# First expert of an attention and mixture-of-experts kernel: its third weight chunk is loaded behind two token gathers, the rest behind five, and the next expert's choices start behind two tiles' remainders

## The chip, the core and the metric

The kernel runs on one core of a Trainium2 chip. The metric is the device time of one execution in microseconds (us), of which a median of some runs is taken. The engines named below are PE (TensorE, matrix products; PEld is its load of stationary operands), DVE (VectorE), ACT (ScalarE), POOL (GpSimd) and SP (SyncE, which here only issues DMAs). POOL issues DMAs too. In the DMA tables q1 holds what SP issues and q0 (software_dynamic) what POOL issues.

## The reference, cut to what matters

```python
attn_out = _attn_ref(q, k, v)          # 8 x 8 heads, 576 positions, window of 64
x = attn_out.transpose(0, 2, 1, 3).reshape(4608, 512)
logits = x @ w_gate                    # 8 experts
order = np.argsort(-logits.flatten())
for idx in order:                      # best pair first
    tok, e = idx // 8, idx % 8
    if assigned[tok] >= 0 or counts[e] >= 576: continue
    assigned[tok] = e; counts[e] += 1
for e in range(8):
    mask = assigned == e
    h = np.maximum(x[mask] @ w1[e], 0.0)   # 512 -> 1024
    out[mask] = h @ w2[e]                  # 1024 -> 512
```

Each expert gets exactly 576 tokens, given out greedily by descending score, so the experts are settled one after another: an expert's tokens are known once the threshold score at which it fills up is found, with all earlier experts' tokens taken out.

## The kernel before

The first part computes attention and writes its rows to a buffer `xs` in device memory. The second part, which the change concerns, has three interwoven strands for each expert p = 0 to 7.

**Routing** (`Routing.steps`). On DVE the *choices* (L772, L554 to L561) find each token's best expert that is left. ACT copies the result into `one4` (L782). Then eight *rounds* (`search`) narrow the threshold: DVE compares (`G`, L586), PE counts (nine products, L632), DVE picks the next digit. A list of the token numbers follows (`listing`: products L911 or L909, L921), and its last step writes `idx` (L927). Expert 0 has a shorter search of its own (`first`).

**Loading** (`Experts.load`). An expert's weights come in eight chunks of 512 KB (128 x 1024 floats): 0 to 3 of w1, 4 to 7 of w2. Each is loaded into `st` (L993). ACT rounds it to `wh` (L1016) and writes `wl` = -`wh` (L1030), and an adding DMA of POOL's queue adds `st` to `wl` (L1032), which leaves the rounding error in `wl`. Expert 0's chunk 0 takes a subtraction on DVE (L1044) in place of the adding DMA. Before the change expert 0's chunks 0 to 3 are issued by SP and 4 to 7 by POOL.

**Tokens and products** (`Experts.turn`, `Experts.steps`). POOL gathers the tokens in five indirect DMAs (L1085): four tiles of 128 rows into `xg` and a last one of 64 into `rest`. PE transposes each tile (`tp`, four products, L1104), ACT rounds it to `xh` (L1074) and DVE writes the remainder beside it (L1078; *remainders* or *lows* in the code). Products of expert 0 (`h`, L1166) come in units of twelve: four of `wh` with the rounded tokens, four of `wl`, four of `wh` with the remainders. A unit needs 128 columns of a weight chunk, so two units need one chunk. The first six units (chunks 0 to 2) take the first 256 tokens, then the same six take the other 320, then chunk 3's. ACT writes each unit's result to `hh` (L1130) and DVE its remainder to `hl` (L1135); three buffers `h` go round. The second layer is `o` (L1200, L1210), and a scatter of POOL's queue writes the rows out (L1189). Where PE has nothing to do at the start, small products of no use keep it busy (`warm`, L593): 28 behind expert 0's list and 6 behind its first tile.

The order on each engine is fixed when the program is written out. Generators wait in a queue (`Streams`) under a clock that is a guess of times, and the instruction of the earliest goes down next. So the guessed times (`there`, `ADDED`, `GATHER` and so on) set which instruction stands ahead of which, and every engine then works strictly through its list.

Of the kernel before, what the change touches and what calls it, by code (L numbers as in the profile page):

```python
# [444 lines left out]
class Routing:  # L445
# [316 lines left out]
    def steps(self, p):  # L762

        nc, wk, V = self.nc, self.wk, self.V
# [5 lines left out]
        if p < E - 1:  # L770
            if p:
                for f in self.choices(0, NJ, p):  # L772
                    f()
                    yield self.dve(490)
# [16 lines left out]
            q = tile_([128, NJ], FT, name="q")  # L791
# [70 lines left out]
    def listing(self, p, Y, slack):  # L862

        nc = self.nc
# [34 lines left out]
        for j0, j1 in ((0, NJ),) if p else ((0, 18), (18, 36)):  # L899
            n = j1 - j0  # L900
# [22 lines left out]
        if p == 0:  # L923
            self.warm(28)
        yield self.busy(255) + 200 + slack
# [17 lines left out]

GATHER = 4200
PLAIN, ADDING, TOKENS, LAND, FETCH = 1350, 2650, 700, 2000, 3600
ADDED = 4500
# [5 lines left out]
class Experts:  # L952
    def __init__(self, ctx, tc, c, xs, w1, w2, out, ring=8):
# [11 lines left out]
        self.first = 0  # L965
        self.gathered = 0
        self.sent = 0
        self.turned = 0
# [12 lines left out]
    def load(self, p, ei):  # L981
# [7 lines left out]
        def fetch(i):  # L989
            st[i] = fw.tile([128, 1024], FT, name="st", bufs=STAGE)  # L990

            q, r = (nc.gpsimd, eg) if p == 0 and i >= 4 else (nc.sync, e)
            q.dma_start(st[i], self.part(i, r))  # L993

            t = self.clock() + self.busy(PLAIN, "dma") + (LAND if i else FETCH)
            if p == 0:
                t = max(self.clock(), there.get(i - 1, 0)) + 1500 * (1 if i else 2)
            if p == 0 and i == 4:

                t = max(t, self.clock() + self.busy(0, "pool") + FIRST)  # L1000
            there[i] = t

        ahead = 3 if p else 4
        for i in range(ahead):
            fetch(i)
        if p == 0:
            yield lambda: self.gathered
        for i in range(2 * NCH):
# [10 lines left out]
            if not (p and quick):  # L1019
                yield lambda: self.gathered > p  # L1020
            if p == 0 and i == 0:
# [6 lines left out]
            else:  # L1028

                nc.scalar.activation(lo, hi.bitcast(FT), AF.Copy, scale=-1.0)  # L1030
                yield self.busy(1050, "act") + 100
                nc.gpsimd.dma_start(lo.bitcast(FT), st[i], accum_op=OP.add)  # L1032
                t = self.busy(650, "pool")
                t = max(t + 350 + ADDING, self.busy(ADDING, "dma")) + LAND if p else t + ADDED - 1200
                self.spawn(self.ready(p, i, hi, lo), t)
                dt = 1300
            self.taken += 1
            for n in () if p == 0 and i < 2 else (4, 5, 6) if p == 0 and i == 2 else (i + ahead,):
                if n < 2 * NCH:
                    fetch(n)  # L1040
# [22 lines left out]
    def turn(self, p, idx):  # L1063
# [18 lines left out]
        g = [g[:, a] for a in range(4)] + [self.rest]  # L1082
        for a in range(5):
            n = 128 if a < 4 else 64
            nc.gpsimd.indirect_dma_start(out=g[a][0:n], out_offset=None, in_=self.xs,  # L1085
                                         in_offset=IndirectOffsetOnAxis(ap=idx[0:n, a:a + 1], axis=0))
            self.busy(TOKENS, "dma")
        if not p:
            self.begun = self.clock()
        self.gathered += 1  # L1090
        there = self.clock() + self.busy(6400, "pool") + GATHER
        yield lambda: self.first == p
        self.XT[p] = x = fw.tile([128, NX, 2 * CAP], FR, name="xh")
        for tiles in ((0, 1), (2, 3), (4,)) if p else ((0,), (1,), (2,), (3,), (4,)):
            yield max(0, there - 1280 * (4 - tiles[-1]) - self.clock())
            if p > 1:
# [4 lines left out]
            for n, a in enumerate(tiles):  # L1101
# [4 lines left out]
                self.spawn(evac(a, 128 if a < 4 else 64, t), dt + 150 + 700 * n)  # L1106
            if p == 0 and a < 1:
                self.warm(6)
# [144 lines left out]
def body(tc, q, k, v, vt, wg, w1, w2, xs, out):  # L1253
    nc = tc.nc
    with ExitStack() as ctx:
# [10 lines left out]
        ex = Experts(ctx, tc, c, xs, w1, w2, out)  # L1266
        rt.spare, rt.joined = ex.room, ex.join

# [44 lines left out]
```

## Time and profile before

| | |
|---|---|
| median of three runs | 632.21 us (628.75 to 632.36) |
| the profiled execution | 634.6 us, of which its span is 632.8 us |
| PE busy over the span | 601.8 us (95%), 5968 products |
| DVE, ACT, POOL busy | 457.6, 371.5 and 188.0 us |
| mean granted clock of PE | 0.982 of full speed |

The profiled execution took 1.8 us more than its span, and 2.4 us more than the median. The span is read in stages: attention up to some 152 us, expert 0's routing up to 168 us, and then the eight experts. Where PE works without a gap, a stage is as long as PE's own list of instructions; where it has a gap, the last wait in front of the gap sets the time.

### The profile page before, as it was taken

How to read it: one execution, taken by the hardware profiler on the slowest of the kernel's cores; microseconds unless marked ns; L12 is line 12 of the kernel's file. 1: busy time of each engine (PE TensorE's matmuls, PEld its weight loads, DVE VectorE, ACT ScalarE, POOL GpSimd, SP SyncE). 2: the span in 40 equal slices, each digit the busy share in tenths (PEclk: the TensorE clock that was granted, in tenths of full speed). 3: DMA queues.
4: the chain of work that ended last, by engine and by line, in shares of the span. 5: the costliest groups of instructions: out<-in, count | busy, mean ns of one | idle time of the engine just before them, and what ended most of it. 6: DMA issues, size and time to landing. Idle time of an engine off the chain costs nothing.

```text
span 632.8 us, 16208 instructions
## 1 busy us (share of the span) xinstructions
PE 601.8 (95%) x5968; PEld 512.4 (81%) x5968; DVE 457.6 (72%) x2151; ACT 371.5 (59%) x798; POOL 188.0 (30%) x244
## 2 busy tenths in 40 slices
PE   8999999996589999999999999999999999999996
PEld 6677777885489878878988997898889779888984
DVE  6888888887678869877986897798789646714410
ACT  6788888996365177357636735564664536514310
POOL 1324453341241162045107204420621460011011
PEclk9999999998689999999999999999999999999999
DMA  9999999942597199379829927983994798210001
GB/s 318 332 364 366 370 388 385 347 159 73 184 235 157 47 320 244 74 258 231 195 89 291 247 58 272 221 191 117 252 230 86 277 242 304 67 41 35 2 25 51
DMA packets 44945, 128.82 MB, mean 204 GB/s; under 512 B 4672, under 2 KB 5312, under 8 KB 44864
## 3 DMA queue, kind: packets, MB, share of 16 engines
q1 hardware_dynamic: 30736, 79.52, 35.1%
q0 software_dynamic: 13840, 47.72, 32.5%
q8 instruction: 48, 0.79, 0.5%
q10 hardware_dynamic: 288, 0.52, 0.3%
q14 instruction: 33, 0.27, 0.1%
HBM read 82.14 MB, written 18.87 MB: 160 GB/s over the span
## 4 chain that ended last, share of the span: by engine, by line
PE 52%; issue 17%; DMA 2%; POOL 2%; DVE 2%; ACT 1%; another core or an unknown queue 0%; POOLq 0%; DVEq 0%
PE h L1166 25%; PE o L1210 18%; PE o L1200 4%; PE rps L632 2%; DMA wl<-st 2%; POOL out L1189 2%; PE tp L1104 2%; PE rps L593 1%; PE rps L909 1%; DMA xs<-x 0%; ACT xh L1074 0%; DVE xh L1078 0%; PE rps L911 0%; POOLq L1309 0%
## 5 line engine op out<-in xcount | busy, mean ns | idle before, releaser
L1166 PE MATMUL h<-xh,wh 128*128 128x320 f32 (+2 forms) x800 | 161.9, 334 | 1.8 <-ACT xh L1074 1.8
L1166 PEld LDWEIGHTS h<-xh,wh 128*128 128x128 f32 x800 | 125.2, 190 | 6.7 <-ACT xh L1074 1.9
L1189 POOL DMA_INDIRECT out<-ot,idx x40 | 42.2, 1055 | 244.9 <-DVE ot L1187 98.2
L1210 PE MATMUL o<-wh,hh 128*128 128x512 f32 x256 | 101.2, 395 | 0.0
L1210 PE MATMUL o<-wh,hl 128*128 128x512 f32 x256 | 100.9, 394 | 0.0
L1210 PE MATMUL o<-wl,hh 128*128 128x512 f32 x256 | 100.7, 393 | 0.0
L141 ACT ACTIVATE pe<-st,mx 128x128 f32<-128x128 f32 x288 | 92.0, 393 | 5.9 <-DVE mx L136 5.8
L1166 PE MATMUL h<-xh,wl 128*128 128x256 f32 (+1 forms) x512 | 92.1, 299 | 0.0
L1166 PEld LDWEIGHTS h<-xh,wl 128*128 128x128 f32 x512 | 79.3, 189 | 4.4
L136 DVE CUSTOM_DVE_ANT_0 st<-Sp,mask 128x128 f32<-128x128 f32 x288 | 63.8, 285 | 8.2 <-PE Sp L128 7.2
L1016 ACT ACTIVATE wh<-st 128x1024 fp32r<-128x1024 f32 x64 | 67.4, 1054 | 2.8 <-DMA st<-w 2.8
L1032 POOL DMA_DIRECT2D wl<-st x51 | 46.3, 976 | 64.5 <-ACT wl L1030 23.6
L1180 ACT ACTIVATE ot<-o 128x512 f32<-128x512 f32 x32 | 19.1, 597 | 75.2 <-PE o L1210 68.6
L1210 PEld LDWEIGHTS o<-wh,hl 128*128 128x128 f32 x256 | 48.1, 188 | 9.5
L1210 PEld LDWEIGHTS o<-wl,hh 128*128 128x128 f32 x256 | 48.1, 188 | 9.5
L1210 PEld LDWEIGHTS o<-wh,hh 128*128 128x128 f32 x256 | 48.1, 188 | 9.2
L1030 ACT ACTIVATE wl<-wh 128x1024 fp32r<-128x1024 f32 x51 | 53.9, 1057 | 0.6
L1127 DVE TENSOR_TENSOR sum<-h,sum 128x256 f32<-128x256 f32 x56 | 23.3, 415 | 37.3 <-ACT sum L1125 36.7
L1130 ACT ACTIVATE hh<-h 128x320 fp32r<-128x320 f32 (+1 forms) x72 | 30.9, 430 | 29.1 <-PE h L1166 28.2
L150 ACT ACTIVATE pt<-Tp 128x512 f32<-128x512 f32 x72 | 42.2, 588 | 9.8 <-PE Tp L148 9.6
L176 PE MATMUL Op<-VO,pt 128*64 128x73 f32 x608 | 43.3, 230 | 3.4 <-issue 2.9
L176 PEld LDWEIGHTS Op<-VO,pt 128*64 128x64 f32 x608 | 37.6, 136 | 8.3 <-issue 3.7
(207 smaller groups left out, 1095.9 us busy)
## 6 DMA issues: line engine op xcount, KB each, us to landing
st<-w SPq DMA_DIRECT2D x60, 512.0 KB
wl<-st POOLq DMA_DIRECT2D x51, 512.0 KB
xs<-x SPq DMA_DIRECT2D x36, 256.0 KB
VO<-v SPq DMA_DIRECT2D x6, 1168.0 KB
Q<-q SPq DMA_DIRECT2D x6, 1152.0 KB
K<-k SPq DMA_DIRECT2D x6, 1152.0 KB
VT<-vt SPq DMA_DIRECT2D x6, 1152.0 KB
VO<-v SPq DMA_DIRECT2D x4, 584.0 KB
```

The source lines that it names most:

```text
L136: nc.vector.tensor_tensor_reduce(st[:, h, :], Sp[h % 2][:, h // 2], mk, scale=-0.125, scalar=3.0e38, op0=OP.add, op1=OP.min, accum_out=mx[ ...
L141: nc.scalar.activation(pe[:, h, :], st[:, h, :], AF.Exp, bias=mx[:, h:h + 1], scale=-1.0)
L150: return pt, lambda: nc.scalar.activation(pt.rearrange("p h q -> p (h q)"), Tp, AF.Copy)
L176: nc.tensor.matmul(Op[g][64 * a:64 * a + 64, h, :], pt[:, h, 64 * a:64 * a + 64], vv[a][:, 4 * g + h, :], start=True, stop=True)
L1016: nc.scalar.activation(hi, st[i], AF.Copy)
L1030: nc.scalar.activation(lo, hi.bitcast(FT), AF.Copy, scale=-1.0)
L1032: nc.gpsimd.dma_start(lo.bitcast(FT), st[i], accum_op=OP.add)
L1130: nc.scalar.activation(hh[:, f, c0:c1], h, AF.Relu)
L1166: nc.tensor.matmul(h[:, 0:w], wv[:, cc, 128 * (f % 2):128 * (f % 2) + 128], x[:, cc, x0:x0 + w], start=(k == 0), stop=(k == 4 * len(terms) ...
L1189: nc.gpsimd.indirect_dma_start(out=self.out[5 * p + a], out_offset=IndirectOffsetOnAxis(ap=idx[0:m, a:a + 1], axis=0), in_=ot[0:m], in_off ...
L1200: nc.tensor.matmul(o, hh[:, f, 512:], w[:, 512 * (f % 2):512 * (f % 2) + 512], start=(f == 0 and n == 0), stop=(f == NF - 1 and n == 1))
L1210: nc.tensor.matmul(o, ht[:, f, 128 * a:128 * a + 128], wt[:, 512 * (f % 2):512 * (f % 2) + 512], start=(k == 0), stop=(k == 23))
```

## The change

- `load`: for expert 0, SP issues chunks 0 and 1 alone. Chunk 2 is issued by POOL once two gathers have been issued (`got > 1`), and chunks 3 to 6 by POOL once chunk 2 has been handled.
- `turn`: for expert 0, two gathers are issued first; the other three wait until one adding DMA has been issued (`added`). The guessed times of the tiles are written out anew.
- `steps` of the routing: expert 1's choices wait until two tiles' remainders stand in DVE's list (`begin`).
- `warm`: 17 in place of 28 behind expert 0's list, and 6 behind the second tile as well as the first.

```diff
@@ Routing.steps
             if p:
+                if p == 1:
+                    yield self.begin
                 for f in self.choices(0, NJ, p):
@@ Routing.listing
-            self.warm(28)
+            self.warm(17)
@@ Experts.load
-            q, r = (nc.gpsimd, eg) if p == 0 and i >= 4 else (nc.sync, e)
+            q, r = (nc.gpsimd, eg) if p == 0 and i >= 2 else (nc.sync, e)
...
+            if p == 0 and i == 2:
+                t = self.clock() + SECOND_CHUNK
...
-        ahead = 3 if p else 4
-        for i in range(ahead):
+        ahead = 3
+        for i in range(ahead if p else 2):
             fetch(i)
         if p == 0:
-            yield lambda: self.gathered
+            yield lambda: self.got > 1
+            fetch(2)
...
-                yield lambda: self.gathered > p
+                yield lambda: (self.got > 1 if i < 2 else self.gathered) if p == 0 else self.gathered > p
...
                 nc.gpsimd.dma_start(lo.bitcast(FT), st[i], accum_op=OP.add)
+                self.added += 1
...
-            for n in () if p == 0 and i < 2 else (4, 5, 6) if p == 0 and i == 2 else (i + ahead,):
+            for n in () if p == 0 and i < 2 else (3, 4, 5, 6) if p == 0 and i == 2 else (i + 4 - (p > 0),):
@@ Experts.turn
-        for a in range(5):
+        def get(a):
             n = 128 if a < 4 else 64
             nc.gpsimd.indirect_dma_start(...)
             self.busy(TOKENS, "dma")
-        if not p:
+            self.got += 1
+        def others():
+            yield lambda: self.added
+            for a in range(2, 5):
+                get(a)
+            self.gathered += 1
+            self.busy(3900, "pool")
+        for a in range(2 if p == 0 else 5):
+            get(a)
...
+                yield lambda: self.gathered or a0 < 2
+                yield max(0, there + (0, 1100, 5000, 6300, 7600)[a0] - self.clock())
...
-            if p == 0 and a < 1:
+            if p == 0 and a < 2:
                 self.warm(6)
@@ body
-        rt.spare, rt.joined = ex.room, ex.join
+        rt.spare, rt.joined, rt.begin = ex.room, ex.join, lambda: ex.lows[0] > 1
```

Three places show how the lists move. First POOL's list at expert 0's gathers, before (numbers behind a name tell buffers apart; `st_3953` is chunk 1 and `st_3955` chunk 2, both loaded by SP):

```order
L1085 DMA xg_4043<-xs,idx0_4041 128x512 x4
L1085 DMA rest_3483<-xs,idx0_4041 64x512
L1032 DMA wl_4064<-st_3953 128x1024
L1032 DMA wl_4082<-st_3955 128x1024
L993 ISA
L993 DMA st_4103<-w2 128x1024
```

The same place after (`st_4031` is chunk 2, `st_4136` chunk 3):

```order
L1095 DMA xg_4028<-xs,idx0_4026 128x512 x2
L998 ISA
L998 DMA st_4031<-w1 128x1024
L1040 DMA wl_4048<-st_3953 128x1024
L1095 DMA xg_4028<-xs,idx0_4026 128x512 x2
L1095 DMA rest_3483<-xs,idx0_4026 64x512
L1040 DMA wl_4101<-st_4031 128x1024
L998 ISA
L998 DMA st_4136<-w1 128x1024
L998 ISA
L998 DMA st_4138<-w2 128x1024
```

Chunk 2's load and chunk 1's adding DMA now stand between the second and the third gather, and chunk 3's load stands behind chunk 2's adding DMA.

ACT's list from expert 0's first rounded tile on, before (`st_3957` is chunk 3, `one4` the copies for the first round of expert 1):

```order
L1016 ACTIVATE wh_4081<-st_3955 128x1024
L1030 ACTIVATE wl_4082<-wh_4081 128x1024
L1074 ACTIVATE xh_4049<-tp_4087 128x4x128
L1074 ACTIVATE xh_4049<-tp_4110 128x4x128
L1074 ACTIVATE xh_4049<-tp_4127 128x4x128
L782 COPY one4_4116<-one_75 128x384 x3
L1130 ACTIVATE hh_4053<-h_4118 128x256
L1074 ACTIVATE xh_4049<-tp_4152 128x4x128
L1016 ACTIVATE wh_4160<-st_3957 128x1024
```

The same place after:

```order
L1083 ACTIVATE xh_4033<-tp_4080 128x4x128
L1024 ACTIVATE wh_4100<-st_4031 128x1024
L1160 ACTIVATE hh_4037<-h_4094 128x256
L1038 ACTIVATE wl_4101<-wh_4100 128x1024
L1160 ACTIVATE hh_4037<-h_4112 128x256
L1083 ACTIVATE xh_4033<-tp_4147 128x4x128
L1160 ACTIVATE hh_4037<-h_4130 128x256
L1083 ACTIVATE xh_4033<-tp_4166 128x4x128
L1024 ACTIVATE wh_4177<-st_4136 128x1024
L784 COPY one4_4171<-one_75 128x384 x3
L1083 ACTIVATE xh_4033<-tp_4186 128x4x64
L1038 ACTIVATE wl_4178<-wh_4177 128x1024
```

Chunk 2 is now handled behind the first two tiles and around the first unit's result (`h_4094`), and chunk 3's rounding stands ahead of the copies `one4`, which stood ahead of it before.

PE's list at the change from expert 0's second layer to expert 1's first, before:

```order
L1104 MATMUL tp<-identr,xg 128x128 x8
L1210 MATMUL o<-wh,hh 128x512
...
L1104 MATMUL tp<-identr,xg 128x128 x8
L1210 MATMUL o<-wh,hh 128x512
L1210 MATMUL o<-wl,hh 128x512
L1210 MATMUL o<-wh,hl 128x512
L1166 MATMUL h<-xh,wh 128x512 x4
```

The same place after:

```order
L1134 MATMUL tp<-identr,xg 128x128 x8
...
L1134 MATMUL tp<-identr,xg 128x128 x8
L1196 MATMUL h<-xh,wh 128x512 x4
L1196 MATMUL h<-xh,wl 128x256
L1134 MATMUL tp<-identr,rest 128x128 x4
```

Between the list's last products (L921, now L923) and expert 1's first product there stood 43 products of the second layer; now 27 stand there, all of them ahead of the transposes. PE's first counting round of expert 1 moved as well: it stood behind 22 products `h` and three tiles' transposes, and stands behind 59 and all five tiles'.

## Rows read from the trace of the kernel before

**Rows 1.** The page's head: span of the profiled execution.

```profile
span 632.8 us, 16208 instructions
```

**Rows 2.** Waits of PE from 176 us to the end: total, times, longest.

```profile
PE h L1166 <- ACT xh L1074: 1.8, 1, 1.8
```

**Rows 3.** PE's timeline, 167.5 to 177: start, duration, group, idle before.

```profile
167.70 4.70 PE L593 MATMUL rps<-r,ones 128*128 128x288 bf16 x28
...
173.33 0.51 PE L1104 MATMUL tp<-identr,xg 128*128 128x128 f32 x4 [0.52 <-issue]
...
174.33 0.55 PE L1104 MATMUL tp<-identr,xg 128*128 128x128 f32 x4
176.65 0.69 PE L1166 MATMUL h<-xh,wh 128*128 128x256 f32 x2 [1.77 <-ACT xh L1074]
```

**Rows 4.** Busy time by stretch; the last three columns are PE's clock, DMA share, GB/s.

```profile
170.00:176.70 6.70, 4.16 (x36) 3.13 (x33) 5.20 (x12) 3.96 (x5) 5.79 (x8) 1.00 0.77 226
176.80:180.20 3.40, 3.40 (x18) 3.40 (x19) 1.98 (x5) 1.28 (x3) 1.44 (x3) 0.50 1.06 193
```

**Rows 5.** POOL's timeline, 150 to 245: the first two gathers and the last.

```profile
168.28 1.01 POOL L1085 DMA_INDIRECT xg<-xs,idx  x1 [11.92 <-DVE eq L833]
169.60 1.07 POOL L1085 DMA_INDIRECT xg<-xs,idx  x1 [0.30 <-issue]
...
173.56 1.11 POOL L1085 DMA_INDIRECT rest<-xs,idx  x1 [0.30 <-issue]
```

**Rows 6.** DMA queues, 170 to 172: packets, MB, share.

```profile
q0 software_dynamic: 91, 0.31, 60.7%
```

**Rows 7.** ACT's timeline, 150 to 245.

```profile
175.51 1.08 ACT L1074 ACTIVATE xh<-tp 128x512 fp32r<-128x512 f32 x2 [2.61 <-PE tp L1104]
...
179.41 1.33 ACT L782 COPY one<-one 128x384 bf16<-128x384 bf16 x3
180.64 0.38 ACT L1130 ACTIVATE hh<-h 128x256 fp32r<-128x256 f32 x1
...
181.40 1.07 ACT L1016 ACTIVATE wh<-st 128x1024 fp32r<-128x1024 f32 x1
```

**Rows 8.** PE's timeline, 153 to 200: two groups of products at full clock.

```profile
183.47 1.12 PE L1166 MATMUL h<-xh,wh 128*128 128x256 f32 x8
184.43 0.64 PE L1166 MATMUL h<-xh,wl 128*128 128x256 f32 x4
```

**Rows 9.** The chain of waits, 160 to 185: a round, a tile's transposes.

```profile
181.74 0.27 PE rps L632 x9
182.01 0.35 PE tp L1104 x4
```

**Rows 10.** POOL's timeline, 197 to 206: chunk 7's adding DMA, the last of expert 0.

```profile
197.88 0.86 POOL L1032 DMA_DIRECT2D wl<-st  x1 [2.66 <-ACT wl L1030]
```

**Rows 11.** Busy time by stretch, behind that DMA.

```profile
199.40:202.20 2.80, 2.80 (x30) 2.76 (x29) 2.59 (x11) 0.79 (x2) 0.00 (x0) 1.00 0.93 178
202.20:204.00 1.80, 1.80 (x15) 1.80 (x14) 1.59 (x9) 0.42 (x2) 0.00 (x0) 1.00 0.00 0
```

**Rows 12.** DMA in all: 176.4 to 182.2 (two adding DMAs), 182.4 to 186.6 (three loads).

```profile
DMA packets 259, 0.99 MB, mean 171 GB/s; under 512 B 17, under 2 KB 17, under 8 KB 259
DMA packets 464, 1.66 MB, mean 395 GB/s; under 512 B 62, under 2 KB 62, under 8 KB 463
```

**Rows 13.** PE's timeline, 224 to 240: list's end, second-layer products, third and fourth tile's transposes.

```profile
224.32 0.23 PE L921 MATMUL rps<-s,ils 72*32 72x5 bf16 x8
...
225.28 0.40 PE L1210 MATMUL o<-wh,hl 128*128 128x512 f32 x1
...
231.20 0.39 PE L1210 MATMUL o<-wl,hh 128*128 128x512 f32 x1
...
235.15 0.80 PE L1104 MATMUL tp<-identr,xg 128*128 128x128 f32 x8
```

**Rows 14.** POOL's timeline, 150 to 245: expert 1's fourth gather.

```profile
229.41 0.94 POOL L1085 DMA_INDIRECT xg<-xs,idx  x1 [0.30 <-issue]
```

More of the change, by code (lines that the diff above doesn't have):

```diff
@@ L944 @@
 GATHER = 4200
+GOT = 3200
+SECOND_CHUNK = 5300
 PLAIN, ADDING, TOKENS, LAND, FETCH = 1350, 2650, 700, 2000, 3600
@@ L966, in __init__ @@
         self.gathered = 0
+        self.got = self.added = 0
         self.sent = 0
@@ L1087, in turn @@
             self.busy(TOKENS, "dma")
-        if not p:
+            self.got += 1
[7 more added lines that the diff above has]
+            get(a)
+        if p:
+            self.gathered += 1
+            there = self.clock() + self.busy(6400, "pool") + GATHER
+        else:
             self.begun = self.clock()
-        self.gathered += 1
-        there = self.clock() + self.busy(6400, "pool") + GATHER
+            self.busy(2600, "pool")
+            there = self.begun + GOT
+            self.spawn(others())
         yield lambda: self.first == p
@@ L1094, in turn @@
         for tiles in ((0, 1), (2, 3), (4,)) if p else ((0,), (1,), (2,), (3,), (4,)):
-            yield max(0, there - 1280 * (4 - tiles[-1]) - self.clock())
+            a0 = tiles[0]
+            if p:
+                yield max(0, there - 1280 * (4 - tiles[-1]) - self.clock())
+            else:
+                yield lambda: self.gathered or a0 < 2
+                yield max(0, there + (0, 1100, 5000, 6300, 7600)[a0] - self.clock())
             if p > 1:
```

## Prediction

> **What bounds the kernel now.** I read the waits of PE first, over everything behind 176 us. There is one entry that concerns the stage of the change: PE's first product of expert 0 waits 1.8 us for ACT's rounding of the tokens [rows 2]. Behind it PE's list runs nearly without gaps to the end, so what moves PE's first product, or opens a gap later, moves the end by as much. Second, PE's timeline in front of that wait [rows 3]: 28 fillers run up to 172.4, the first tile is transposed at 173.33, the second at 174.33, and the first product starts at 176.65. Third, the stretches with the clock [rows 4]: full speed (2.4 GHz) from 170 to 176.7, half (1.2 GHz) from 176.8 to 180.2, right behind the idle time in front of the first product. So 3.4 us of products did 1.7 us of work. Those are the two things that the change can win here: the wait and the slow stretch. The rest is what the new lists may lose. The sum is made against the profiled execution, 634.6 us (span 632.8 [rows 1] and 1.8 around it); the median of the runs is 2.4 below that, and the same difference is laid on it.
>
> **The start (A).** Before, the first gather's issue ends at 169.29 and the second's at 170.67 [rows 5]; their order and issue stay. What goes is the competition: SP's chunks 2 and 3, 1 MB, no longer share the DMA engines with them. POOL's queue had moved 0.31 MB by 172.0 [rows 6], more than the first gather's 0.26 MB, so its data was there at 172.0 at the earliest, and 173.33 is when PE used it. The 17 fillers take 17/28 of 4.70 us, a little more as the first are the slow ones: they end at about 170.9, and no longer stand in the way. I take the first tile at 172.3, the second 1.4 later by the distance of the issues, 173.7; its transposes take 0.5, its rounding 0.6 (half of 1.08 [rows 7]), so the first product could stand at 174.8. One thing I can't explain: ACT began at 175.51, 1.7 us after the first tile's transposes end in the timeline at 173.84 [rows 3, 7]. If this pause stays whole the first product stands at 176.3; if it goes, with the earliest data, at 174.5. I take 175.1, near the middle of the upper half, since the pause has no cause that the change touches but the traffic. A is 175.1 - 176.65 = **-1.55** (-2.15 to -0.35).
>
> **The slow stretch (B).** With six more fillers behind the second tile the idle time in front of the first product shrinks from 1.77 to about 0.6 us. But the shorter first batch leaves PE idle from 170.9 to 172.3, and the same fall may follow that. A fall that came 3.4 us earlier would end at 176.8 and hit only the products from 175.1 on, 0.85 us lost in place of 1.7. Between a gain of 1.7 and none I take **-1.2**, since most of a shifted stretch lies ahead of the products. The Trainium skill, "TensorE: Matmul & The Clock Gate", Part 1, says that the slow clock is the default and activity releases it, which by the fillers alone would give B = -1.7, and would make the wait in C below cost a full slow stretch, D = +1.7: the sum would be 3.25 in place of 2.85.
>
> **The wait at the first counting round (C).** Here the new lists lose. In ACT's list chunk 3's rounding now stands ahead of the copies `one4`, and chunk 3's load stands in POOL's queue behind chunk 2's adding DMA, which itself waits for ACT's `wl` of chunk 2, which stands behind the first unit's `hh`. From the first product on, in us: the first unit, 12 products at 0.12 (eight start in 0.96 [rows 8]), 1.44; `hh` 0.38 [rows 7]; `wl` 1.07 (as `wh`, the same shape [rows 7]); issue of the adding DMA 0.86 [rows 10]; its transfer from 198.74 to 202.20 with an idle queue ahead, 3.46 [rows 10, 11]; chunk 3's load, 0.52 MB at 395 GB/s, 1.33 [rows 12]; `wh` 1.07; three copies 1.33 [rows 7]; the last third of the count, 0.2. That is 11.1. PE comes to the end of this round by its own list after 59 products at 0.12, three tiles at 0.35 and the round's 0.27 [rows 8, 9]: 8.4. It waits 2.7. Behind the copies ACT has still to round the last tile (0.4), write chunk 3's `wl` (1.07) and the fourth unit's `hh` (0.38), and the seventh unit needs that buffer: PE reaches it 13 products (1.56) after the round, ACT and DVE some 0.5 later. C is **+3.2**. Lower end 1.5: the load needs nothing of its own behind the adding DMA, and the second wait hides. Upper end 4.2: a microsecond for the landing behind the transfer, which these rows don't show. Before, the same chain was harmless, since chunk 3 was in its buffer long before ACT took it at 181.40 without waiting, and the copies were done at 180.74 [rows 7].
>
> That loads come one behind another on POOL's queue is read from rows 12: the two adding DMAs moved 0.99 MB at 171 GB/s, and only then the three loads ran at 395. The Trainium skill, "DMA: Bandwidth & Descriptors", section "SWDGE vs HWDGE vs iDMA", speaks against this part of the change: plain loads belong to SP or ACT, whose descriptors go to other queues inside the DMA engines than POOL's, and the engines take turns between them. By that a chunk 3 left on SP would not have stood behind the adding DMA at all, C would be near 0 and the sum -0.35; no run so far shows the one beside the other.
>
> **A slow stretch behind the wait (D).** An idle time of 1.77 us was followed by 3.4 us at half speed; 2.7 us may be too. It costs 0 or 1.7; **+0.8**.
>
> **Expert 1's start (E).** Its routing starts behind two tiles' remainders, and its rounds stand later among the products: from the list's last products to expert 1's first there are 27 second-layer products in place of 43, so 16 x 0.23 = 3.7 us less cover (26 products from 225.28 to 231.20 [rows 13]). Before, the transposes of the third and fourth tile stood at 235.15, 10.8 behind the list's end at 224.32 [rows 13]; now PE reaches them after 27 x 0.23, eight transposes and a round, 7.4. The fourth gather's issue ends 6.03 after the list's end (230.35 [rows 14]). A gather lands 2.7 (172.0 - 169.29 above) to 4.0 us after its issue (from 169.29 to 173.33, when PE used it [rows 3, 5]). So the data is there at 8.7 to 10.0, and PE waits 1.3 to 2.6. I take **+1.6**, near the end at which the gather isn't disturbed, and 0 as the lower end, if `idx` is ready sooner against PE.
>
> **What costs nothing.** POOL's other list changes: the last gather's issue moves from 174.67 to about 176.5, and the last tile is needed by the seventh unit, ten microseconds after the first product. The w2 chunks land some 3 us later and are first needed 28 us after the first product; the last adding DMA was done at 202.2 and its data is used at about 209.7, so 7 us of cover stand against that. DVE's later choices end before ACT's copies can start, because of C; without C they would decide the first round. Past expert 1 the routing had time to spare.
>
> **Sum.** -1.55 - 1.2 + 3.2 + 0.8 + 1.6 = +2.85. The profiled time would be 637.5, the median 635.1. All lower ends together give -2.35 (629.9), all upper ends +8.15 (640.4).
>
> **Rivals.** First, the gain stands: chunk 3 is there when ACT comes to it, 5.8 us behind the first product, because the load overtakes the adding DMA. For it speaks that nothing in the rows forbids two transfers side by side; against it that rows 12 show them one by one. C and D go: -1.15, 631.1. Second, slower by over 1%: chunk 2's own load comes late. It stands behind two gathers on POOL's queue, and the chain of C starts at the first unit's result only if chunk 2 has landed by about 175.8. Each microsecond beyond moves ACT's `wl`, chunk 3 and the copies by one, with PE behind. At 4 us, which it takes if the gathers and chunk 2 move at the adding DMA's 171 GB/s, the sum is +6.85, 639.1. Against it: loads ran at 395. Third, the change doesn't do what it says: the gathers are paced by POOL's issue and land no sooner, so A and B are nothing and the losses stay: +5.6, 637.8.
>
> **Chances.** The forecast 0.55, the standing gain 0.27, late chunk 2 0.10, no sooner gathers 0.08. 1% is 6.3 us, about what a measurement of this kernel can tell from no change. Faster by more than that only a tail of the first rival: 0.04. Slower by more: most of the second, some of the forecast's upper end and of the third: 0.15. Within: 0.81. The range of 8 in 10 takes in the standing gain with E at nothing (629.5) and late chunk 2: 629.5 to 639.5.
>
> **What would show it.** Right: PE's first product at about 175.1; ACT's rounding of chunk 3 waits some 3 us for the load `st`, with the copies right behind; PE's first round of expert 1 waits for them; the transposes of expert 1's third tile wait. Wrong: no wait of ACT on `st` there, or a first product before 174.5 or not before 176.5, or a stretch at half speed in another place. The forecast falls most easily with C: it rests on transfers of one queue following each other.

## The result, and the profile after

The changed kernel took **638.89 us** (median of six, 636.77 to 643.65) beside 632.29 for the kernel before on the same chip: ratio 1.0135, interval 1.0098 to 1.0171, so 1.4% slower. On another chip it was 638.65 beside 629.61, ratio 1.015 (1.0119 to 1.0181). The forecast was 635.1 and no change that can be told.

The profiled execution has a span of 641.2 us in place of 632.8 [rows 1]; it was the longest of the six (643.65). Its waits of PE from 176 to 250 us (total, times, longest), where before the longest was one of 1.8 [rows 2]:

```profile
PE rps L632 <- ACT one L784: 2.0, 3, 1.7
PE h L1196 <- DMA wl<-st: 1.5, 1, 1.5
PE tp L1134 <- DVE xh L1087: 1.0, 1, 1.0
PE tp L1134 <- PE tp L1134: 0.4, 1, 0.4
```

PE's timeline at the start of expert 0, after (L1134 is the transposes, L1196 the products `h`, L923 the list's last products):

```profile
168.49 4.26 PE L593 MATMUL rps<-r,ones 128*128 128x288 bf16 x17
172.69 0.69 PE L1134 MATMUL tp<-identr,xg 128*128 128x128 f32 x4
...
174.61 0.90 PE L593 MATMUL rps<-r,ones 128*128 128x288 bf16 x6
175.42 0.73 PE L1196 MATMUL h<-xh,wh 128*128 128x256 f32 x4
...
184.47 0.74 PE L1196 MATMUL h<-xh,wl 128*128 128x256 f32 x4 [1.49 <-DMA wl<-st]
185.06 0.52 PE L1196 MATMUL h<-xh,wh 128*128 128x256 f32 x3
187.28 1.16 PE L632 MATMUL rps<-G,one 128*128 128x60 bf16 x9 [1.70 <-ACT one L784]
```

The start did what was forecast. The first tile is transposed 4.2 us behind the first filler, before 5.6 [rows 3], and the first product stands at 6.9 in place of 8.95, with no idle time ahead of it. Then PE waits twice, 3.2 us in all. The chain of waits of the same kernel tells why the second is so long:

```profile
178.80 0.07 POOL wl L1040
...
179.39 6.35 DMA st<-w
...
185.76 1.06 ACT wh L1024
186.82 1.23 ACT one L784 x3
...
188.10 0.33 PE rps L632 x3
```

The same place in the timelines of POOL and of ACT:

```profile
178.78 0.97 POOL L1040 DMA_DIRECT2D wl<-st  x1 [1.85 <-ACT wl L1038]
179.39 2.52 POOL L998 DMA_DIRECT2D st<-w  x4
...
185.76 1.06 ACT L1024 ACTIVATE wh<-st 128x1024 fp32r<-128x1024 f32 x1 [4.36 <-DMA st<-w]
```

POOL issues chunk 2's adding DMA and behind it chunk 3's load, which lands 6.35 us later; ACT waits for it with the copies of expert 1's first round behind it. This is the chain of step C. Next the stretches with the clock (length, PE busy, PEclk, DMA share, GB/s), after:

```profile
176.80:180.20 3.40, 3.40 (x32) 1.00 0.64 213
...
186.90:193.70 6.80, 6.26 (x32) 0.50 0.76 198
193.70:241.50 47.80, 46.74 (x333) 1.00 0.60 166
241.50:248.30 6.80, 6.13 (x32) 0.50 1.05 203
```

The half speed of [rows 4] is gone from the first units. Two longer stretches at 1.2 GHz have come, one behind the waits of expert 0, one at expert 1's start. Half of the busy time in them is what they cost: 3.1 and 3.1 us. Expert 1's start after, in PE's timeline:

```profile
232.07 0.23 PE L923 MATMUL rps<-s,ils 72*32 72x5 bf16 x8
...
241.79 0.75 PE L1134 MATMUL tp<-identr,xg 128*128 128x128 f32 x4 [0.96 <-DVE xh L1087]
242.92 0.72 PE L1134 MATMUL tp<-identr,xg 128*128 128x128 f32 x4 [0.38 <-PE tp L1134]
243.44 2.04 PE L1196 MATMUL h<-xh,wh 128*128 128x512 f32 x4
```

The list stands 63.6 us behind the first filler, before 56.6 [rows 13]. Of these seven microseconds 6.3 add up: the earlier start (-2.0), PE's waits in expert 0 (3.2), the slow stretches (3.1 in place of 1.7) and the 16 second-layer products that stood behind the list and now stand ahead of it (3.7, at 0.23 [rows 13]). Which edit causes what of this is what the experiments had to find out.

### The profile page after: what moved, and what is told of

Same layout as the page of the kernel before. It is cut to its first block, busy times and chain, and to the rows that moved or that the text cites. A ratio compares the mean times of both kernels' runs of the same rounds, so it can differ in the third digit from the quotient of the medians.

```text
span 641.2 us, 16196 instructions
## 1 busy us (share of the span) xinstructions
PE 607.5 (95%) x5963; PEld 515.9 (80%) x5963; DVE 459.3 (72%) x2151; ACT 371.3 (58%) x798; POOL 189.5 (30%) x246
## 4 chain that ended last, share of the span: by engine, by line
PE 51%; issue 17%; POOL 3%; DMA 2%; ACT 1%; DVE 0%; POOLq 0%
PE h L1196 24%; PE o L1240 20%; PE o L1230 3%; PE rps L632 2%; DMA st<-w 2%; POOL out L1219 2%; PE tp L1134 2%; POOL xg L1095 1%; PE rps L911 1%; POOL wl L1040 0%; ACT one L784 0%; DMA xs<-x 0%; PE rps L913 0%; ACT ot L1210 0%; POOLq L1339 0%
## 5 line engine op out<-in xcount | busy, mean ns | idle before, releaser
L1196 PE MATMUL h<-xh,wh 128*128 128x320 f32 (+2 forms) x800 | 164.2, 338 | 0.0
L1196 PEld LDWEIGHTS h<-xh,wh 128*128 128x128 f32 x800 | 126.7, 192 | 5.0 <-ACT xh L1083 0.2
L1196 PE MATMUL h<-xh,wl 128*128 128x256 f32 (+1 forms) x512 | 93.1, 301 | 1.5 <-DMA wl<-st 1.5
L1196 PEld LDWEIGHTS h<-xh,wl 128*128 128x128 f32 x512 | 80.2, 191 | 6.2 <-DMA wl<-st 1.7
L1024 ACT ACTIVATE wh<-st 128x1024 fp32r<-128x1024 f32 x64 | 67.3, 1052 | 6.5 <-DMA st<-w 6.3
## 6 DMA issues: line engine op xcount, KB each, us to landing
VT<-vt SPq DMA_DIRECT2D x6, 1152.0 KB, 16.1
```

Of the source, the lines that this page charges most:

```text
L1024: nc.scalar.activation(hi, st[i], AF.Copy)
L1196: nc.tensor.matmul(h[:, 0:w], wv[:, cc, 128 * (f % 2):128 * (f % 2) + 128], x[:, cc, x0:x0 + w], start=(k == 0), stop=(k == 4 * len(terms) ...
```

## The experiments

All times below are beside the kernel before on the same chip. One table carries the argument: for each profiled execution five moments in us behind its first filler (starts in PE's timeline, less the start of the first L593 of the stage; the last column is the span's end).

| kernel | ratio (interval) | first product | first round | list | expert 1's first product | end |
|---|---|---|---|---|---|---|
| before | 1 | 8.95 | 13.9 | 56.6 | 68.9 | 465.1 |
| before_again | | 8.65 | 12.1 | 54.8 | 67.2 | 463.0 |
| keep_before | 0.9997 (0.9976-1.0019) | 8.5 | 11.4 | 55.0 | 67.3 | 463.5 |
| late_round | 1.0013 (0.999-1.0036) | 9.4 | 15.25 | 57.3 | 68.1 | 465.1 |
| warm_only | 0.9991 (0.997-1.0011) | 10.5 | 14.8 | 57.5 | 69.75 | 465.7 |
| begin_only | 1.0122 (1.0082-1.0163) | 8.4 | 18.4 | 60.5 | 71.6 | 469.8 |
| changed kernel | 1.0135 (1.0098-1.0171) | 6.9 | 18.8 | 63.6 | 74.9 | 472.75 |
| again | 1.015 (1.0119-1.0181) | 6.7 | 18.6 | 62.45 | 73.65 | 470.5 |
| early3 | 1.0134 (1.0109-1.0159) | 7.0 | 20.2 | 61.9 | 73.1 | 470.2 |
| fill | 1.0109 (1.0092-1.0127) | 6.75 | 18.6 | 61.25 | 72.65 | 469.3 |
| sp23 | 1.0107 (1.0068-1.0147) | 8.9 | 19.8 | 61.5 | 72.9 | 469.8 |
| one_first | 1.0063 (1.0044-1.0081) | 6.7 | 16.1 | 57.5 | 68.2 | 465.4 |
| sp23_first | 1.0056 (1.0026-1.0085) | 9.2 | 18.5 | 59.2 | 69.9 | 467.0 |
| no_begin | 1.0052 (1.0033-1.007) | 6.7 | 13.6 | 57.85 | 68.6 | 465.8 |
| mend | 1.0027 (1.0002-1.0052) | 6.75 | 14.8 | 56.1 | 67.0 | 463.9 |
| mend4 | 1.0023 (1.0002-1.0045) | 6.7 | 13.6 | 55.2 | 65.9 | 463.1 |
| mend5 | 1.0053 (1.0026-1.008) | 6.7 | 12.8 | 57.5 | 68.6 | 466.0 |

**again** and **before_again**: both kernels unedited, for second profiles.

> The changed kernel once more, unedited: a second profile and a second set of times, since its profiled execution (643.65 us) was the longest of six. It showed two stretches at half clock behind waits of PE (6.8 us from 186.9, 6.8 us from 241.5), each worth some 3 us. If they belong to the kernel, both are there again and the time is 637 to 640; if they are an accident of that execution, at least one is missing from this profile, the mean clock is 0.98 or more, and the span is 3 to 6 us shorter than 641.

> The kernel before, unedited, for a second profile: its profiled execution (634.6 us) was longer than its median, by 2.4 us there and 4 to 5 us beside the later runs, and showed 3.4 us at half clock in front of the first units. If that stretch belongs to the kernel it is there again; if it is an accident of the execution, it is missing, the mean clock is 0.984 or more, and the span some 2 us under 632.8. In the second case the term for the slow stretch in the prediction had nothing to win in most executions.

Waits of PE in *again* from 176 to 250 us, and its one slow stretch (length, PE busy, PEclk, DMA share, GB/s):

```profile
PE rps L632 <- ACT one L784: 2.0, 3, 1.7
PE h L1196 <- DMA wl<-st: 1.3, 1, 1.3
PE tp L1134 <- DVE xh L1087: 1.0, 1, 1.0
PE tp L1134 <- DMA xg<-xs,idx: 0.8, 1, 0.8
PE rps L632 <- DVE G L586: 0.6, 1, 0.6
PE tp L1134 <- PE tp L1134: 0.6, 1, 0.6
...
187.20:190.50 3.30, 3.30 (x16) 0.50 0.51 113
```

The waits of expert 0 are there again (1.3 and 1.7 us) and those at expert 1's start are longer (2.4 in place of 1.6). Of the two stretches at half clock one is left, of 3.4 us, and none stands at expert 1's start; the mean clock is 0.981, and the median time is 638.65. So the waits in expert 0 belong to the kernel, while the slow stretches behind them differ from one execution to the next. In *before_again* the first units run at full speed:

```profile
176.70:180.20 3.50, 3.50 (x41) 1.00 1.06 191
```

So the half clock of [rows 4] belonged to that execution (mean clock 0.982; of 90 other timed executions of the kernel before 85 have 0.984 or more), and so did ACT's pause ahead of the rounding [rows 7]: here ACT rounds the first tile at 174.28, right behind its transposes of 173.73.

**early3**: chunk 3's load ahead of the adding DMAs.

```diff
-            fetch(2)
+            fetch(2); fetch(3)
...
-            for n in () if p == 0 and i < 2 else (3, 4, 5, 6) if p == 0 and i == 2 else ...
+            for n in () if p == 0 and i < 2 else (4, 5, 6) if p == 0 and i == 2 else ...
```

> Chunk 3's load is issued right behind chunk 2's, ahead of the adding DMAs of chunks 1 and 2 and of the last three gathers; nothing else moves, on no engine. Theory A (what holds PE up at expert 1's first round is ACT, which waits 4.4 us for chunk 3's load, since that load follows chunk 2's adding DMA on POOL's queue): ACT no longer waits there, PE's wait of 1.7 for the copies goes, and the fall of the clock behind it too, so 1.7 to 5 us are won (634 to 637). Theory B (POOL's queue simply carries too much at the start): the 0.5 MB are moved to the front and the third tile, chunk 1's adding DMA or chunk 2's come 1.3 us later in their place, so the gain is under 1 us. Theory C (the loss sits at expert 1's start and is due to its later choices): within 1 us of the changed kernel, with the waits there untouched.

Theory B came true. ACT no longer waits for chunk 3, but chunk 1's adding DMA and the third gather come later, and PE waits for them in place of the round, 3.0 us in all as in *again*:

```profile
180.04 0.38 PE L1196 MATMUL h<-xh,wl 128*128 128x256 f32 x1 [2.58 <-DMA wl<-st]
180.81 0.54 PE L1134 MATMUL tp<-identr,xg 128*128 128x128 f32 x4 [0.39 <-DMA xg<-xs,idx]
```

A place further ahead in POOL's queue is taken from what stands behind.

**fill**: products of no use in PE's idle times.

```diff
+            if p == 0 and u == 4: self.fill(h[:, 0:288], 12)
...
+            if p == 1 and r == 0: self.fill(cf, 13)
...
+                if p == 1 and 1 < a < 4: self.fill(self.room()[:, 0:288], (12, 6)[a - 2])
```

> The changed kernel with small products of no use put in where PE waited: 12 ahead of expert 0's fifth unit (some 1.4 us), 13 ahead of expert 1's first round (1.6 us), 12 and 6 ahead of the transposes of expert 1's third and fourth tile (1.4 and 0.7 us). The lists are otherwise the same. If idle time of PE is what makes the clock fall, the waits stay as long as before, filled, and the two stretches at half clock behind them are gone or shorter: 3 to 6 us less than the changed kernel, 633 to 636. If the clock falls for another reason (or the fillers only lengthen PE's list), the time is equal or up to 2 us longer, and the half clock stretches stay.

Measured: 636.21, 2.4 us less than the changed kernel in the same session, with no slow stretch from the fillers to expert 1:

```profile
168.10:190.00 21.90, 21.34 (x179) 1.00 0.88 235
190.00:250.00 60.00, 58.86 (x430) 1.00 0.73 190
```

With the idle time filled the clock doesn't fall: all five executions have a mean clock of 0.983, the six of *again* 0.970 to 0.981, the kernel before 0.983 to 0.987 on that chip. This is worth 2.4 us of the 9.0 in the median, or some 3: the fillers take a little more than the waits did (first product to expert 1's first 65.9 us, in *again* 66.9 of which 1.7 are lost at half clock). The other 6 are not the clock.

**one_first** and **no_begin**: first ACT's order alone (chunk 3's rounding behind the last tile), then no wait of expert 1's choices.

```diff
@@ one_first
-                yield lambda: self.tiles[0] > 3
+                yield lambda: self.tiles[0] > 4
@@ no_begin
-                if p == 1:
-                    yield self.begin
```

> Chunk 3's rounding on ACT moves behind the three copies for expert 1's first round and behind the last tile; its load stays where the change put it. Theory A in its narrow form (ACT's order alone makes the wait): PE's wait of 1.7 at the round goes; the wait of 1.5 for chunk 2's adding DMA stays, and a new wait for chunk 3 itself comes at the seventh unit, at most 1 us; 1 to 4 us less than the changed kernel. If the load's lateness counts whatever ACT's order is, PE waits at the seventh unit for as long as it now waits at the round, and the time is within 1 us of the changed kernel.

> The changed kernel without the wait of expert 1's choices for two tiles' remainders. Its three copies stand ahead of chunk 3's rounding on ACT again, and 43 second-layer products stand between expert 1's list and its first product as before. Theory E (the later choices cost both at the first round and at expert 1's start): both waits go, 1.7 and 1.6 us, and with them the falls of the clock behind them; 4 to 7 us less than the changed kernel, 631 to 635 where that takes 638.7. If the loads alone make the loss, PE waits as long for chunk 3 or chunk 2 somewhere among expert 0's units, and the time is within 2 us of the changed kernel.

Measured: each takes some 6 us off the changed kernel (ratio 1.015 to 1.0063 and 1.0052) and leaves the wait for chunk 2's adding DMA (1.3 and 1.1 us); no wait for chunk 3 comes in place of the one at the round. What both have in common is the first round, at 16.1 and 13.6 in place of 18.6, some 0.5 us of idle time ahead of expert 1's first product in place of 2.4, and no stretch at half clock. But *no_begin* stays 0.5% above before although its first product comes 1.9 us sooner; PE waits there 1.1 us for the adding DMA, 1.2 for `hl` and 1.0 for `G`.

**sp23** and **sp23_first**: the loads of chunks 2 and 3 on SP, as before, without and with *one_first*'s edit.

```diff
-            q, r = (nc.gpsimd, eg) if p == 0 and i >= 2 else (nc.sync, e)
-            q.dma_start(st[i], self.part(i, r))
+            q, r = (nc.gpsimd, eg) if p == 0 and i >= 4 else (nc.sync, e)
+            if i not in held: q.dma_start(st[i], self.part(i, r))
...
-        for i in range(ahead if p else 2):
+        for i in range(ahead if p else 4):
...
+        if not p: held = (2, 3)
```

> The changed kernel with the loads of chunks 2 and 3 back on SP, issued right behind chunks 0 and 1 as before; every other instruction on every engine stands where the change put it. Theory Q (the loss at expert 0 comes from POOL's queue, through which two loads, five gathers and the adding DMAs go one behind another): ACT no longer waits for chunk 3, the adding DMAs of chunks 1 and 2 land a microsecond or more sooner, PE's waits of 1.3 to 1.7 us in front of the first round and for wl go; the first product comes 1 to 2 us later than in the changed kernel, since the loads share the engines with the first gathers again. Sum: 2 to 5 us less than the changed kernel. Theory R (the loads cost the same whichever queue takes them): the first product comes 2 us later and nothing else is won, 1 to 2 us more than the changed kernel.

> Both mends together: loads of chunks 2 and 3 on SP as before, and chunk 3's rounding on ACT behind the copies. If the queue's load (theory Q) and ACT's order each cause a part of the loss, this is the fastest of the changed kernels, with no wait over 0.7 us in expert 0: 1 to 3 us less than with ACT's order alone (which took 633.1 beside 629.6 for the kernel before). If ACT's order was all of it at the round, it equals that kernel plus what the first product loses, 633 to 635.

Measured: the early start is the loads' doing. With them on SP again the first tile comes late, everything else standing as in the changed kernel:

```profile
166.01 4.26 PE L593 MATMUL rps<-r,ones 128*128 128x288 bf16 x17
171.96 0.51 PE L1135 MATMUL tp<-identr,xg 128*128 128x128 f32 x4 [1.69 <-issue]
```

ACT's wait for chunk 3 and PE's at the round go (the one for chunk 2's adding DMA stays, 1.5 us), yet the first round, as far down PE's list as in the changed kernel and behind a later start, is no sooner (19.8). The ratio goes from 1.015 to 1.0107, and as the intervals overlap this isn't told from no change. *sp23_first* has 1.0056, as *one_first*: the queue of the loads is no large part.

**warm_only**: 17, 6 and 6 fillers in the kernel before.

> The kernel before with the fillers alone changed: 17 in place of 28 behind the list, 6 behind the second tile too. If the 28 fillers hold the first tile up, its transposes come up to 1 us sooner, the pause in front of the first product is filled, the clock does not fall there: 1 to 2.7 us less than before. If the first tile's data is what PE waits for (before, it was there at 172.0 at the earliest, and the fillers ended at 172.4), the first product stays within 0.3 us of its place and the time within 1 us of before.

Measured: no change. The first tile's transposes wait 3.2 us for the gather's data there; the 28 fillers held nothing up.

**begin_only**: the later choices alone, in the kernel before.

```diff
+                if p == 1: yield self.begin
                 for f in self.choices(0, NJ, p):
```

> The kernel before with one edit of the change: expert 1's choices wait for two tiles' remainders. Loads, gathers and fillers are as before, and chunk 3 is in its buffer early. Theory E (the later choices alone make expert 1's start late): PE waits 1 to 2 us at expert 1's third and fourth tile, 1 to 3 us more than before. If the loss at expert 1's start comes only from the waits in expert 0, no change within 0.7 us.

Measured: 638.33 beside 630.66. Alone this edit costs about as much as the whole change. But alone it also does more than within the change: the first round stands behind 73 products `h` (22 before, 59 in the changed kernel), and 20 second-layer products are left behind the list (43 before, 27 in the changed kernel). What it costs within the change is what *no_begin* gives back, some 1%, the wait at the round and the clock with it. PE's timeline at the first round, 179.42 in *before_again*:

```profile
184.82 0.55 PE L632 MATMUL rps<-G,one 128*128 128x60 bf16 x6
```

Its waits of PE from 176 to 250 us that are longer than 0.3:

```profile
PE tp L1105 <- issue: 1.9, 2, 1.4
PE tp L1105 <- DVE xh L1079: 1.1, 1, 1.1
PE tp L1105 <- PE tp L1105: 0.5, 1, 0.5
```

Its clock at expert 1's start:

```profile
236.70:243.50 6.80, 5.95 (x31) 0.50 1.05 201
```

Expert 0 runs undisturbed, with no wait for a load. PE comes to the first round 6.3 us later than in *before_again*; the list comes 5.7 later, expert 1's first product 4.4, and PE idles 3.6 us ahead of that product and loses 3.0 more (half of 5.95) at half clock.

**late_round** and **keep_before**: in the kernel before the first round alone, later and sooner.

```diff
@@ late_round
-                    yield 1500
+                    yield 3500
@@ keep_before
-            if 0 < p < E - 2:
+            if p < E - 2:
```

> The kernel before with the copies for expert 1's first round, and the round itself, some 2 us later (13 products further down PE's list); choices, loads, gathers and fillers as before. Theory R (the routing chain that begins at this round sets expert 1's start): the list and expert 1's first product come 1.5 to 2 us later and PE idles that much there; 1.5 to 2.5 us more than before, up to 5 if the clock falls behind the idle time. Theory P (PE's own list sets it, the routing has slack): within 0.6 us of before.

> The kernel before with one small sum of the routing (how many tokens expert 0 took) put behind expert 1's first round, as it is for the later experts: DVE doesn't wait for PE there, the choices start sooner, and the first round stands 8 products, about 1 us, further up PE's list. If the routing chain alone sets expert 1's start, 1 us or more less than before. If PE's list is as tight as the chain in the kernel before (its idle time at expert 1's start was 0.4 us or less), within 0.6 us of before.

Measured: neither theory whole. 3.1 us later cost 0.8 us by the ratio, not told from nothing; 0.7 sooner won nothing. So the first round had some 3 us to spare in the kernel before; *begin_only* takes 6.3 and pays. Where between the two the cost begins isn't shown.

**mend**, **mend4**, **mend5**: the early start with what stood in its way taken out.

```diff
@@ mend: no_begin and one_first, and
-        return p == 0 and i < 1 or ...
+        return p == 0 and i in (0, 2) or ...
@@ mend4: mend and keep_before, and
-                    yield 1500
+                    yield 0
```

*mend5* is *mend4* with chunk 2's adding DMA.

> The changed kernel with three things mended: no wait of expert 1's choices, chunk 3's rounding on ACT behind the last tile, and chunk 2's rounding error subtracted on DVE (as chunk 0's) in place of an adding DMA, so chunk 3's load stands right behind the last gather. What is left of the change: two gathers ahead of chunks 2 and 3, and the fillers. If the three named waits are the whole loss, PE waits nowhere over 0.7 us in expert 0, the first product is still 2 us sooner than before against the list, and the time is 1 to 2.5 us under the kernel before. If the loss has another part that no wait shows, it stays 1 us or more above the kernel before.

> The mended kernel (earlier choices, chunk 3 behind the last tile, chunk 2's error on DVE), with that sum moved too and the copies 1.5 us sooner: the first round should come at 12 to 13 us from the first filler in place of 14.8. Theory R: 2 us less than the mended kernel, which puts it 0.5 to 1.5 us under the kernel before. Theory P: the same time as the mended kernel, 1 to 2 us above before.

> As mend4, but chunk 2's error again by the adding DMA, so that DVE and ACT come to the choices and copies sooner; first round at 11 to 12 us from the first filler. Theory R: what the earlier round wins is paid in part by the wait for chunk 2's adding DMA (1.1 to 1.5 us in the runs with it); within 1 us of before. Theory P: that wait comes on top, 1.5 to 3 us above before.

Measured: *mend* has no wait left in expert 0; PE's waits from 165 to 250 us are all at expert 1's start:

```profile
PE tp L1134 <- issue: 1.3, 1, 1.3
PE rps L632 <- DVE G L586: 0.9, 1, 0.9
PE tp L1134 <- PE tp L1134: 0.5, 1, 0.5
```

It isn't faster than before (ratio 1.0027), nor is *mend4*, whose expert 1 starts 1.3 us sooner than in *before_again* and whose end is equal: from there to the end it takes 397.2 us in place of 395.8, and 1.1 of this is a wait of the next round for `G`, which *before_again* doesn't have; the other 0.3 was not found. *mend5*'s second round is late (20.7), behind waits for chunk 2's adding DMA and `hl`. No kernel with the early start is faster than the kernel before.

## Why the prediction was wrong

**What failed: the terms for the clock, B and D, and that none stood behind E.** Together the prediction put them at -1.2 + 0.8 = -0.4 us. Between the two first profiles they came to -1.7 + 3.1 + 3.1 = +4.5, between the two second ones to +1.7, and in the median of the changed kernel the falls of the clock are worth 2.4 us or some 3 (*fill*). The prediction took the slow stretch of [rows 4] for something that every execution has, so that there was 1.2 to win, and for the measure of what a wait costs, 3.4 us long; and it let no stretch follow on the idle time of E. One of its own signs of being wrong came: a stretch at half speed in another place, at 241.5 us. The sum fell short by some 4.7 us in either pair. In the first the clock is all of this (4.9); in the second it is 2.1, and E stands 0.7 above its forecast, other rounds wait 0.9 more, and 1.5 are not assigned. The terms for PE's start and its idle time, A, C and E, held within their ranges. In us:

| term | forecast | *before* to *after* | *before_again* to *again* |
|---|---|---|---|
| A, first product | -1.55 | -2.0 | -1.9 |
| B, slow stretch before | -1.2 | -1.7 | 0 |
| C, waits in expert 0 | +3.2 | +3.2 | +3.0 |
| D, slow stretch behind them | +0.8 | +3.1 | +1.7 |
| E, waits at expert 1's start | +1.6 | +1.6 | +2.3 |
| slow stretch behind E | none | +3.1 | 0 |
| other waits of rounds, for `G` and the copies | none | -0.4 | +0.9 |
| sum | +2.85 | +6.9 | +6.0 |
| measured, first filler to end | | +7.6 | +7.5 |

Another 0.8 of the difference of the two first spans lies ahead of the fillers, where nothing was changed. The rests of 0.7 and 1.5 are not assigned. An estimate for most of them: a single product shows 0.28 us, although what follows it starts 0.12 behind it, so that ahead of a wait some 0.16 us in which nothing starts count as busy; the profiles after have six and seven waits more than those before, 1.0 and 1.1 us. The two rows:

```profile
178.86 0.28 PE L1196 MATMUL h<-xh,wl 128*128 128x256 f32 x1
178.98 0.47 PE L1134 MATMUL tp<-identr,xg 128*128 128x128 f32 x4
```

**Why the early start won nothing.** "What moves PE's first product, or opens a gap later, moves the end by as much" left out that here the one opens the other. Beside PE's list runs a chain: eight rounds, the list, the gathers, the transposes. In *before_again* `G` of the first round is ready 2.1 us before PE comes to it (177.34 and 179.42). From the second round to the eighth PE comes within 0.3 us of it; the second one, on DVE and on PE:

```profile
184.28 0.40 DVE L586 TENSOR_TENSOR G<-m,thr 128x240 bf16<-128x240 f32 x1
...
184.66 0.43 PE L632 MATMUL rps<-G,one 128*128 128x60 bf16 x9
```

So between its first round and the list this chain has next to nothing to spare in the kernel before either; what it has lies ahead of the first round and behind the list. From the first round to expert 1's first product it takes 51.4 (*sp23_first*) to 53.2 us (*begin_only*) in the kernels in which PE then waits for it and no stall, filler or slow clock falls among the rounds; in the kernel before it took 55.0 to 55.1, since there PE came last. The second path is PE's own work, 58.5 us from the first product to expert 1's in *before_again*. Expert 1 starts behind the later of the two: before, 12.1 + 52 = 64 beside 8.65 + 58.5 = 67, so PE's list; after, 18.8 + 52 = 71 beside 6.9 + 58.5 + 3.2 (the waits of C) = 69, so the chain; the slow stretch in expert 0 comes on top of both. PE starts 2 us sooner, the first round doesn't, and the gain comes back as idle time at expert 1's start. The prediction had that time in E, from the products left behind the list.

The terms one by one:

- **A**: right, and for the reason given: *sp23* loses it again. That [rows 6] put the first tile's data at 172.0 "at the earliest" doesn't follow, since bytes moved by 172.0 speak for 172.0 at the latest; E's 2.7 us from issue to landing rests on it. In the changed kernel the first gather took 2.4 us from the end of its issue.
- **B**: right between the two first profiles by luck, as the stretch was one execution's; in most there was nothing to win.
- **C**: in sum as forecast, and the chain at the round was the one described (ACT waits 4.36 us for chunk 3). The second wait was in another place: not chunk 3 at the seventh unit, but chunk 2's adding DMA at the fifth. PE was there at 182.98; by the 3.46 us of [rows 10, 11] the transfer, whose issue ended at 179.75, would have been done at 183.2, but PE could use it at 184.47, after 4.7.
- **D**: 3.1 in the first profile after, 1.7 in the second.
- **E**: 1.6 (0.96, 0.38 and twice 0.15), then 2.4 (0.1 of it stands in *before_again* too), both within 0 to 2.6, and found the right way, by the second-layer products left behind the list. In the profiles: 43 products and 0 to 0.1 us of idle time ahead of expert 1's first product (*before*, *before_again*, *keep_before*, *warm_only*), 36 and 0.4 to 0.6 (*late_round*, *no_begin*, *mend5*), 34 or 35 and 0.6 (*one_first*, *sp23_first*, *mend4*), 30 and 1.8 (*mend*), 27 and 1.6 to 2.4 (the changed kernel, *early3*, *sp23*), 20 and 3.6 (*begin_only*). What was missing is the clock behind it, 3.1 us in the first profile, 3.0 in *begin_only*, nothing in *again*.

Of the rivals, the standing gain and the late chunk 2 didn't come: chunk 2's load landed at 175.74, as C assumed. With chunks 2 and 3 on SP the waits for chunk 3 go (*sp23*), but the kernel still loses 1.07%. That is half of what follows from the Trainium skill, "DMA: Bandwidth & Descriptors", section "SWDGE vs HWDGE vs iDMA": C's wait at the round goes as it would have it, and the sum by it, a gain of 0.35, is far off, since the rule bears on the load and not on the round's place. *sp23* has chunk 2 on SP as well and loses A with it; and the sum of -0.35 kept D's 0.8 where no wait was left for it, while the first rival, without both, had -1.15. With PE kept busy (*fill*) no stretch at 1.2 GHz is left behind the first fillers; this agrees with the Trainium skill, "TensorE: Matmul & The Clock Gate", Part 1, by which D would have been 1.7 in place of 0.8.

Open are what is left of the two rests beyond that estimate, and why slow stretches behind equal waits are of unequal length or missing.

## What to carry to other kernels

Where a dense engine works through a list into which a serial chain is woven, write down both paths to the next point where they meet, each with its spare time, before a step of the chain is moved down the list: here some 3 us were to spare and 6.5 were taken (*before_again* to *again*). A gain at the start of one path counts only if the other path moves too. Look at a second execution before a slow stretch of the clock is entered as something to win, and where a new wait of PE is forecast, let a fall of the clock stand behind it as a term of its own, with a range.

## What the runs showed of the hardware

An adding DMA of 512 KB took 3.5 us from the end of its issue with nothing ahead of it or behind it [rows 10, 11], and 4.7 (179.75 to 184.47, when PE used it) with four loads issued right behind it on the same queue and the last gather, which landed at 180.18, still ahead of it. Which of the two slowed it isn't shown. The four loads landed at 185.74, 187.35, 188.63 and 189.93, one behind another.

In the first profile after the clock fell within the wait, at 186.9, 0.4 us ahead of the round that ended it; in *again* it fell at 187.1, 1.5 us behind the start of that round at 185.61. Like waits (1.5 and 1.7 us, 1.3 and 1.7) were followed by 6.8 us at half clock in the one execution and 3.4 in the other; waits of 1.1 to 1.3 in *one_first*, *no_begin* and *mend* by none.
